# One sequence for the first layer: three groups of row-tiled products in place of four, and an earlier transfer of the second half's remainder

## Chip, cores and metric

The kernel runs on one core of one Trainium2 chip; the other cores are idle. The metric is the device time of one execution, in microseconds (us), as the median of several runs. "The span" is the time from the first to the last instruction of one execution taken with the hardware profiler.

## What is computed

Six cross layers over a batch of 4096 rows of 416 features, all in bf16:

```python
def reference(x0, ws, bs):          # x0 4096 x 416, ws 6 x 416 x 416, bs 6 x 416
    x = x0
    for l in range(ws.shape[0]):
        x = x0 * (x @ ws[l] + bs[l]) + x
    return x
```

## The kernel before

**Layout.** For layers 0 to 4 the features lie on the partitions. 416 is three blocks of 128 (`XM`, index `k` as input and `m` as output) and a remainder of 32 (`XR`). The batch is cut into two halves `s` of 2048 rows, each half into four groups `g` of 512. Since 32 features fill a quarter of the partitions only, `XR` keeps the four groups of a half on top of each other: group `g` sits on partitions `32g` to `32g+31`. A second copy, `XRd`, holds the same with its lower and upper 64 partitions exchanged. `XM[0]` and `XR[0]` hold x0; layer 0 writes `XM[1]` and `XR[1]`.

**Products on PE.** An output of 128 features x 1024 rows (a half-block: half `s`, block `m`, `h` = which two of the four groups) is one PSUM tile of two banks, called `ph` in layer 0 and `pt` in layers 1 to 4. It needs three *full* products for each of its two groups (128 x 128 weights, `k` = 0, 1, 2; L233), and one *row-tiled* product for each group, whose 32 input features take one quarter of the rows of the array (L240). Four row-tiled products in the four different quarters run side by side; this is one round. Output block `m = 1` reads `XRd` instead of `XR[0]`, so that its two products fall into the two quarters which the others leave free. In layers 1 to 4 the main products are *column-tiled* (L200): four products of 32 output features each run side by side and make one round. The remainder's own 32 outputs are column-tiled as well (`mm_rem`, L212 and L217, tile `pr`).

**After PE.** ACT reads a finished PSUM tile, adds the bias and writes `t` in bf16 (L173). DVE multiplies `t` by x0 (L180) and adds x (L183); for the remainder L189 and L192. There are four PSUM tiles of two banks and six `t` buffers, each given out again when its last reader is done.

**The first layer before the change.** `first_layer(s)` runs once for each half. The half begins with the three half-blocks of `h = 0` (`pa`), then comes a group of eight row-tiled products (two rounds), then the three half-blocks of `h = 1` (`pb`), then a group of four (one round). After the second half, `mm_rem` makes the remainder's outputs for both halves in one tile `pr`, and layer 1 starts with the tile pair of `s = 0, m = 0`: `mm_full` for groups 0 and 1 into the first tile of the pair, groups 2 and 3 into the second, then `mm_row`.

**Where the remainder of x0 comes from.** For the first half, four transfers bring it to `xrig` (L83); PE turns it into the tile `tpr` (L159), and DVE copies that to `XR[0]` and twice, by halves, to `XRd` (L162). For the second half, one transfer brings it to `xrem` (`load_xrem1`, L88, on ACT's queue); DVE transposes it to `XR[0]` in blocks of 32 x 32 (L167) and makes two copies to `XRd` (L169). The transfer is kept back by a tiny DVE write to `xrem` (L86), which stands behind the copies of L162 and which the transfer must wait for. The remainder rows of the first layer's weights come by one transfer to 32 partitions of `WR`, and are copied to the other three quarters by ACT (twice, L115) and POOL (L117). Eight transposing transfers on SP's queue (L75) bring x0 to `XM[0]`, one for each group of 512 rows.

`pin` keeps an instruction in the order in which it is written, on its engine. ACT, DVE and PE each take their instructions in one order.

Of the kernel before, what the change touches and what calls it, by code (L numbers as in the profile page):

```python
# [9 lines left out]
ACT = mybir.ActivationFunctionType  # L10
ALU = mybir.AluOpType
BF16 = mybir.dt.bfloat16
# [4 lines left out]
def kernel(  # L17
# [7 lines left out]
    nc = tc.nc  # L25
    B, D = x0.shape
    L = ws.shape[0]
    P = 128
    NK = 3
    R = D - NK * P  # L30
    assert R == 32 and B == 4096 and D == 416 and L >= 2
    NS = 2
    NG = 4
    CW = 512
# [6 lines left out]
    tpool = ctx.enter_context(tc.tile_pool(name="tpool", bufs=6))  # L41
    opool = ctx.enter_context(tc.tile_pool(name="opool", bufs=10))
    psum = ctx.enter_context(tc.tile_pool(name="psum", bufs=4, space=bass.MemoryType.PSUM))
# [7 lines left out]
    WM = const.tile([P, L, NK, D], BF16)  # L51
    WR = const.tile([P, L, D], BF16)
# [3 lines left out]
    bM = const.tile([P, NK, L], FP32)  # L56
    bR = const.tile([P, L], FP32)
# [3 lines left out]
    xrem = big.tile([P, 16, R], BF16)  # L61
    xrig = big.tile([P, 4, P], BF16)
    XRd = big.tile([P, NS * CW], BF16)
    XM = [big.tile([P, NK, B], BF16, name=f"XM{i}") for i in range(3)]
    XR = [big.tile([P, NS * CW], BF16, name=f"XR{i}") for i in range(3)]

    def col0(s, g):
        return SW * s + CW * g
# [8 lines left out]
    def pin(ins):  # L77
        tc.keep_in_program_order(ins)
# [3 lines left out]
            for i in range(4):  # L82
                nc.scalar.dma_start(xrig[:, i, :].rearrange("p (g r) -> p g r", g=NG), x0_v[:, i:16:4, NK * P:D])  # L83

    def load_xrem1():
        pin(nc.vector.memset(xrem[:, 0, 0:1], 0.0))  # L86
        with nc.allow_non_contiguous_dma(reason="64B row segments"):
            pin(nc.scalar.dma_start(xrem[:], x0[SW:2 * SW, NK * P:D].rearrange("(p t) r -> p t r", p=P)))  # L88

# [19 lines left out]
    load_xrem0()  # L109
    load_wr0()  # L110
    nc.scalar.activation(dz[:, 1:2], dz[:, 0:1], ACT.Identity, bias=dz[:, 0:1], scale=1.0)  # L111
    for g in range(1, NG):
        dst, src = WR[32 * g:32 * g + 32, 0, :], WR[0:R, 0, :]
        if g < NG - 1:
            nc.scalar.copy(dst, src)  # L115
        else:
            nc.gpsimd.tensor_copy(dst, src)  # L117
    for g in range(2, NG):
        load_x0t(0, g)
    load_x0t(1, 0)  # L120
# [13 lines left out]
    def fill_wd(l0, l1):  # L134
        for g in range(NG):
            nc.gpsimd.tensor_copy(WD[32 * g:32 * g + 32, l0:l1, g, :], WR[32 * g:32 * g + 32, l0:l1, NK * P:D])

    fill_wd(0, 1)
    fill_wd(1, L)

    wps = psum.tile([P, CW], FP32, tag="ps", name="wps")

# [13 lines left out]
    def x0_rem0(tpr):  # L156
        nc.tensor.transpose(tpr[:, CW:CW + L], bsb[0:L, NK * P:4 * P], ident[0:L, 0:L])
        for i in range(4):
            nc.tensor.transpose(tpr[:, 128 * i:128 * i + 128], xrig[:, i, :], ident[:])  # L159
        for dst, src in ((slice(0, P), slice(0, P)), (slice(64, P), slice(0, 64)), (slice(0, 64), slice(64, P))):  # L160
            to = XR[0] if dst == src else XRd
            pin(nc.vector.tensor_copy(to[dst, 0:CW], tpr[src, 0:CW]))  # L162
        nc.vector.tensor_copy(bR[:], tpr[:, CW:CW + L])
        load_xrem1()

    def x0_rem1():
        pin(nc.vector.transpose(XR[0][:, CW:2 * CW].rearrange("p (j t) -> p t j", t=16), xrem[:]))  # L167
        for dst, src in ((slice(64, P), slice(0, 64)), (slice(0, 64), slice(64, P))):
            pin(nc.vector.tensor_copy(XRd[dst, CW:2 * CW], XR[0][src, CW:2 * CW]))  # L169

    def ew_act(n, pt, bias):
        t = tpool.tile([P, 2 * CW], BF16, name="t")
        nc.scalar.activation(t[:, 0:n], pt, ACT.Identity, bias=bias, scale=1.0)  # L173
        return t

    def ew_main(l, s, m, h, pt, cur, nxt, pin_all=False, t=None):
        c0 = col0(s, 2 * h)
        if t is None:
            t = ew_act(2 * CW, pt[:].rearrange("p a b -> p (a b)"), bM[:, m, l:l + 1])
        prod = nc.vector.tensor_tensor(out=t[:], in0=t[:], in1=XM[0][:, m, c0:c0 + 2 * CW], op=ALU.mult)  # L180
        if pin_all:
            pin(prod)
        total = nc.vector.tensor_tensor(out=nxt[:, m, c0:c0 + 2 * CW], in0=t[:], in1=cur[:, m, c0:c0 + 2 * CW], op=ALU.add)  # L183
        if pin_all and s:
            pin(total)

    def ew_rem(l, s, pr, curR, nxtR, pin_all=False, t=None):
        tr = ew_act(CW, pr, bR[:, l:l + 1]) if t is None else t
        prod = nc.vector.tensor_tensor(out=tr[:, 0:CW], in0=tr[:, 0:CW], in1=XR[0][:, CW * s:CW * s + CW], op=ALU.mult)  # L189
        if pin_all:  # L190
            pin(prod)
        total = nc.vector.tensor_tensor(out=nxtR[:, CW * s:CW * s + CW], in0=tr[:, 0:CW], in1=curR[:, CW * s:CW * s + CW], op=ALU.add)  # L192
        if pin_all:
            pin(total)

    def mm_full(l, s, m, g, pts, cur, first, last):
        c0 = col0(s, g)
        for k in range(NK):
            for q in range(4):
                nc.tensor.matmul(pts[g // 2][32 * q:32 * q + 32, g % 2, :], lhsT=WM[:, l, k, 128 * m + 32 * q:128 * m + 32 * q + 32],  # L200
                                 rhs=cur[:, k, c0:c0 + CW], start=(first and k == 0), stop=(last and k == NK - 1),
                                 tile_position=(0, 32 * q))

    def mm_row(l, s, m, pts, curR, first, last):
        for g in range(NG):
            nc.tensor.matmul(pts[g // 2][:, g % 2, :], lhsT=WR[32 * g:32 * g + 32, l, 128 * m:128 * m + 128],  # L206
                             rhs=curR[32 * g:32 * g + 32, CW * s:CW * s + CW],
                             start=first, stop=last, tile_position=(32 * g, 0))

    def mm_rem(l, s, pr, cur, curR):  # L210
        for g in range(NG):
# [12 lines left out]
        nc.sync.dma_start_transpose(out=XLrows[:, 16 * s:16 * s + 16, 128 * k:128 * k + 128],  # L224
                                    in_=nxt[:, k, SW * s:SW * s + SW])

    def first_layer(s):
        cur, curR, nxt, nxtR = XM[0], XR[0], XM[1], XR[1]

        def full(pt, m, h, gl, after_row):  # L230
            c0 = col0(s, 2 * h + gl)
            for k in range(NK):
                nc.tensor.matmul(pt[:, gl, :], lhsT=WM[:, 0, k, 128 * m:128 * m + 128], rhs=cur[:, k, c0:c0 + CW],  # L233
                                 start=(k == 0 and not after_row), stop=(k == NK - 1 and after_row))

        def row(pt, m, h, opens):
            for gl in range(2):
                rg = 32 * ((2 * h + gl) ^ (2 if m == 1 else 0))
                src = XRd if m == 1 else curR
                nc.tensor.matmul(pt[:, gl, :], lhsT=WR[rg:rg + 32, 0, 128 * m:128 * m + 128],  # L240
                                 rhs=src[rg:rg + 32, CW * s:CW * s + CW],
                                 start=opens, stop=not opens, tile_position=(rg, 0))

        def ph(m):
            return psum.tile([P, 2, CW], FP32, tag="ps", name=f"ph{m}")

        pa = [ph(m) for m in range(NK)]
        if s == 0:
            for m in range(NK):
                full(pa[m], m, 0, 0, False)  # L250
            tp0 = psum.tile([P, CW + 8], BF16, tag="ps", name="tpr")
            x0_rem0(tp0[:])
            for m in range(NK):
                full(pa[m], m, 0, 1, False)
        else:
            for gl in range(2):
                for m in range(NK):
                    full(pa[m], m, 0, gl, False)
        pb = [ph(0)]
        row(pa[0], 0, 0, False)  # L260
        row(pb[0], 0, 1, True)
        row(pa[2], 2, 0, False)
        row(pa[1], 1, 0, False)
        for m in range(NK):
            ew_main(0, s, m, 0, pa[m], cur, nxt, pin_all=(s == 1))
        for m in range(NK):
            if m:
                pb.append(ph(m))
            for gl in range(2):
                full(pb[m], m, 1, gl, m == 0)  # L270
        row(pb[1], 1, 1, False)
        row(pb[2], 2, 1, False)
        if s == 0:
            x0_rem1()
            for m in range(NK):
                ew_main(0, s, m, 1, pb[m], cur, nxt, pin_all=True)
            return
        pr = psum.tile([P, 2, CW], FP32, tag="ps", name="pr")
        for r in range(NS):
            mm_rem(0, r, pr[:, r, :], cur, curR)  # L280

        def act_main(m):
            return ew_act(2 * CW, pb[m][:].rearrange("p a b -> p (a b)"), bM[:, m, 0:1])

        tb, tr = [act_main(0), act_main(1)], [ew_act(CW, pr[:, 0, :], bR[:, 0:1])]
        tb.append(act_main(2))
        tr.append(ew_act(CW, pr[:, 1, :], bR[:, 0:1]))
        ew_rem(0, 0, None, curR, nxtR, True, tr[0])
        for m in range(NK):
            ew_main(0, s, m, 1, None, cur, nxt, True, tb[m])  # L290
        ew_rem(0, 1, None, curR, nxtR, True, tr[1])

    bias_setup()
    pe_filler(1, CW)
    for s in range(NS):
        first_layer(s)

    def rem_pair(l, cur, curR, nxtR, feeds_last):
        pr2 = psum.tile([P, 2, CW], FP32, tag="ps", name="pr2")
# [13 lines left out]
    for l in range(1, LL):  # L313
# [3 lines left out]
        pts = {}  # L317
# [136 lines left out]
```

## Time and profile before

| | |
|---|---|
| Runs | 130.12, 130.23, 130.55 us; median 130.23 |
| The profiled execution | 130.03 us, of which the span is 128.2 us |
| Granted TensorE clock, mean | 0.995 |
| PE busy | 122.7 us (96%), 1698 products |
| DVE busy | 108.1 us (84%), 196 instructions |
| ACT busy | 86.8 us (68%), 99 instructions |
| DMA | 16.38 MB in 42230 packets, 31034 of them under 512 B |

The share of busy time of PE says only that its products follow each other; the chain of waits says whether another engine holds it up. The profile page gives for each line of the kernel (L233 and so on) the number of instructions, the busy time, the mean duration, and the idle time before them with what ended it.

### The profile page before, as it was taken

Reading aid. Unit: us, or ns where it says so; the run is one execution under the profiler, and the core shown is the slowest. Engines: PE = TensorE matmul, PEld = TensorE weight load, DVE = VectorE, ACT = ScalarE, POOL = GpSimd, SP = SyncE. Lnnn points to the kernel's source line nnn. Section 1 sums busy time; section 2 is a strip of 40 time slices with the busy share of each in tenths; the row PEclk is TensorE's granted clock in tenths of the full one; section 3 lists DMA queues with packets and bytes.
Section 4 is the critical chain, followed back from the end, with each engine's and each line's share of the span. In section 5 each row is a group of like instructions: output and inputs, shape, how many; then the busy total and the mean of one; then the engine's idle time right before and its main releaser. Section 6 shows DMA issues by size and latency. Waiting matters only on the chain.

```text
span 128.2 us, 3995 instructions
## 1 busy us (share of the span) xinstructions
PE 122.7 (96%) x1698; PEld 55.1 (43%) x1698; DVE 108.1 (84%) x196; ACT 86.8 (68%) x99; POOL 5.5 (4%) x18
## 2 busy tenths in 40 slices
PE   7999999999999999999999999999999999999960
PEld 3344343444344444434444434444434445445420
DVE  0033999999999999999999989898989899898991
ACT  0138857878496658857658857658857897569670
POOL 4004000700000000000000000000000000000000
PEclk9999999999999999999999999999999999999997
DMA  3999999999960000000000000000297899987754
GB/s 93 248 233 196 193 222 251 279 332 332 337 202 0 5 0 8 0 0 5 0 5 0 5 0 5 0 0 5 48 160 165 161 134 240 182 269 248 224 183 136
DMA packets 42230, 16.38 MB, mean 128 GB/s; under 512 B 31034, under 2 KB 42212, under 8 KB 42212
## 3 DMA queue, kind: packets, MB, share of 16 engines
q1 hardware_dynamic: 37432, 15.40, 52.8%
q10 hardware_dynamic: 4780, 0.72, 3.7%
q8 instruction: 13, 0.21, 0.7%
q14 instruction: 5, 0.04, 0.1%
HBM read 6.15 MB, written 3.41 MB: 75 GB/s over the span
## 4 chain that ended last, share of the span: by engine, by line
PE 81%; DVE 6%; DMA 6%; ACTq 2%; issue 1%; SPq 1%; ACT 1%; DVEq 0%
PE pt L200 50%; PE ph L233 11%; PE pt L206 5%; PE pr L217 5%; PE py L365 4%; DMA xrig<-in_x_dram 4%; DVE t L393 4%; DVE o L382 2%; DMA out_dram<-o 2%; PE pr L212 2%; PE ph L240 1%; PE py L360 1%; ACTq L83 1%; SPq L383 1%; PE py L371 1%
## 5 line engine op out<-in xcount | busy, mean ns | idle before, releaser
L200 PE MATMUL pt<-XM,WM 128*32 128x512 bf16 x1152 | 65.2, 379 | 0.0
L173 ACT ACTIVATE t<-pt,bM 128x1024 bf16<-128x1024 f32 x48 | 49.6, 1115 | 17.7 <-PE pt L206 17.7
L183 DVE TENSOR_TENSOR XM<-t,XM 128x1024 bf16<-128x1024 bf16 x60 | 41.5, 692 | 3.6
L180 DVE TENSOR_TENSOR t<-t,XM 128x1024 bf16<-128x1024 bf16 x60 | 41.4, 689 | 3.5 <-ACT t L173 3.4
L200 PEld LDWEIGHTS <-WM 128*32 128x32 bf16 x1152 | 29.7, 97 | 33.8 <-issue 5.1
L392 ACT CAST t<-py 128x416 bf16<-128x416 f32 (+1 forms) x23 | 14.8, 643 | 4.7 <-PE py L365 2.5
L233 PE MATMUL ph<-XM,WM 128*128 128x512 bf16 x72 | 16.4, 379 | 0.3 <-DMA XM<-in_x_dram 0.3
L365 PE MATMUL py<-WM,XM 128*128 128x416 bf16 x90 | 16.5, 339 | 0.0
L173 ACT ACTIVATE t<-ph,bM 128x1024 bf16<-128x1024 f32 x12 | 12.6, 1113 | 3.5 <-PE ph L240 3.5
L365 PEld LDWEIGHTS <-XM 128*128 128x128 bf16 x90 | 8.5, 98 | 7.8 <-issue 1.4
L393 DVE TENSOR_TENSOR t<-t,X0rows 128x416 bf16<-128x416 bf16 (+1 forms) x23 | 10.4, 456 | 1.1 <-ACT t L392 1.1
L233 PEld LDWEIGHTS <-WM 128*128 128x128 bf16 x72 | 6.8, 98 | 8.8 <-issue 1.3
L382 DVE TENSOR_TENSOR o<-t,XLrows 128x416 bf16<-128x416 bf16 (+1 forms) x23 | 10.4, 455 | 0.0
L173 ACT ACTIVATE t<-pr,bR 128x512 bf16<-128x512 f32 x10 | 6.4, 685 | 2.9 <-PE pr L217 2.9
L217 PE MATMUL pr<-XM,WM 128*32 128x512 bf16 x120 | 8.2, 379 | 0.0
L206 PE MATMUL pt<-XR,WR 32*128 32x512 bf16 x96 | 7.3, 379 | 0.0
L111 ACT ACT_TABLE_LOAD x1 | 1.3, 1283 | 6.0 <-DMA XM<-in_x_dram 6.0
L192 DVE TENSOR_TENSOR XR<-t,XR 128x512 bf16<-128x512 bf16 x10 | 4.2, 424 | 0.7
L217 PEld LDWEIGHTS <-WM 128*32 128x32 bf16 x120 | 3.2, 97 | 3.2
L145 PE MATMUL wps<-const-float32-1.0 128*128 128x512 f32 x4 | 3.6, 1044 | 0.8 <-PEq L438 0.8
L189 DVE TENSOR_TENSOR t<-t,XR 128x512 bf16<-128x512 bf16 x10 | 4.2, 419 | 0.0
L154 DVE CAST bM<-pb 128x18 f32<-128x18 bf16 x1 | 0.2, 177 | 4.5 <-PE pb L153 4.5
(42 smaller groups left out, 36.7 us busy)
## 6 DMA issues: line engine op xcount, KB each, us to landing
X0rows<-in_x_dram SPq DMA_DIRECT2D x8, 312.0 KB, 7.1
out_dram<-o SPq DMA_DIRECT2D x9, 208.0 KB, 4.2
WM<-in_ws_dram SPq DMA_DIRECT2D x5, 312.0 KB
out_dram<-o SPq DMA_DIRECT2D x13, 104.0 KB, 1.7
X0rows<-in_x_dram SPq DMA_DIRECT2D x4, 208.0 KB, 6.1
WR<-in_ws_dram SPq DMA_DIRECT2D x4, 130.0 KB, 5.2
WM<-in_ws_dram ACTq DMA_DIRECT2D x1, 312.0 KB
XM<-in_x_dram SPq DMA_TRANSPOSE x8, 5.6
```

Source lines behind the costliest of these rows:

```text
L173: nc.scalar.activation(t[:, 0:n], pt, ACT.Identity, bias=bias, scale=1.0)
L180: prod = nc.vector.tensor_tensor(out=t[:], in0=t[:], in1=XM[0][:, m, c0:c0 + 2 * CW], op=ALU.mult)
L183: total = nc.vector.tensor_tensor(out=nxt[:, m, c0:c0 + 2 * CW], in0=t[:], in1=cur[:, m, c0:c0 + 2 * CW], op=ALU.add)
L189: prod = nc.vector.tensor_tensor(out=tr[:, 0:CW], in0=tr[:, 0:CW], in1=XR[0][:, CW * s:CW * s + CW], op=ALU.mult)
L200: nc.tensor.matmul(pts[g // 2][32 * q:32 * q + 32, g % 2, :], lhsT=WM[:, l, k, 128 * m + 32 * q:128 * m + 32 * q + 32], rhs=cur[:, k, c0:c ...
L206: nc.tensor.matmul(pts[g // 2][:, g % 2, :], lhsT=WR[32 * g:32 * g + 32, l, 128 * m:128 * m + 128], rhs=curR[32 * g:32 * g + 32, CW * s:CW ...
L217: nc.tensor.matmul(pr[32 * g:32 * g + 32, :], lhsT=WM[:, l, k, NK * P:D], rhs=cur[:, k, c0:c0 + CW], start=False, stop=(k == NK - 1), tile ...
L233: nc.tensor.matmul(pt[:, gl, :], lhsT=WM[:, 0, k, 128 * m:128 * m + 128], rhs=cur[:, k, c0:c0 + CW], start=(k == 0 and not after_row), sto ...
L365: nc.tensor.matmul(py[:, 0:D], lhsT=cur[:, k, q_cols(q, g)], rhs=WM[:, l, k, :], start=((not closes) and k == 0), stop=(closes and k == NK ...
L382: tc.keep_in_program_order(nc.vector.tensor_tensor(out=o, in0=t, in1=xl, op=ALU.add))
L392: nc.scalar.copy(tv, src)
L393: tc.keep_in_program_order(nc.vector.tensor_tensor(out=tv, in0=tv, in1=X0rows[:, b, :], op=ALU.mult))
```

## The change

The two calls of `first_layer(s)` become one call that issues all twelve half-blocks of layer 0 in one sequence. Its row-tiled products stand in three groups of eight (two rounds each). The second group, issued after 24 full products, holds the last ones of the first half (`pb[1]`, `pb[2]`) and the first ones of the second half (`qa[0]`, `qa[1]`). The third holds the rest. The last half-block (`qb[2]`: s = 1, m = 2, h = 1) is issued after the third group with column-tiled products (`cols`), and `mm_rem` follows it. Most instructions of the first layer, and the products of layer 1's first pair, are pinned.

The tiny DVE write that releases the transfer of `xrem` becomes a copy of one column out of `tpr`, and it moves ahead of the three copies to `XR[0]` and `XRd`. The transfer moves ahead of the two copies of `WR` on ACT's queue. DVE's transpose of `xrem` moves from behind the sixth elementwise instruction of layer 0 to behind the second. One of the two copies to `XRd` that follow it goes to ACT (`x0_rem1_low`). ACT's order at the end of the layer is: tile `qa[2]`, `qb[0]`, first remainder, `qb[1]`, `qb[2]`, second remainder. On DVE the first remainder moves ahead of the half-block `qa[2]`.

```diff
-    def load_xrem1():
-        pin(nc.vector.memset(xrem[:, 0, 0:1], 0.0))
+    def load_xrem1(tpr):
+        pin(nc.vector.tensor_copy(xrem[:, 0, 0:1], tpr[:, 3 * P:3 * P + 1]))
         with nc.allow_non_contiguous_dma(reason="64B row segments"):
             pin(nc.scalar.dma_start(xrem[:], x0[SW:2 * SW, NK * P:D].rearrange("(p t) r -> p t r", p=P)))
...
             nc.tensor.transpose(tpr[:, 128 * i:128 * i + 128], xrig[:, i, :], ident[:])
+        load_xrem1(tpr)
+        copy_wr0()
         for dst, src in ((slice(0, P), slice(0, P)), (slice(64, P), slice(0, 64)), (slice(0, 64), slice(64, P))):
             to = XR[0] if dst == src else XRd
             pin(nc.vector.tensor_copy(to[dst, 0:CW], tpr[src, 0:CW]))
         nc.vector.tensor_copy(bR[:], tpr[:, CW:CW + L])
-        load_xrem1()
 
     def x0_rem1():
         pin(nc.vector.transpose(XR[0][:, CW:2 * CW].rearrange("p (j t) -> p t j", t=16), xrem[:]))
-        for dst, src in ((slice(64, P), slice(0, 64)), (slice(0, 64), slice(64, P))):
-            pin(nc.vector.tensor_copy(XRd[dst, CW:2 * CW], XR[0][src, CW:2 * CW]))
+        pin(nc.vector.tensor_copy(XRd[64:P, CW:2 * CW], XR[0][0:64, CW:2 * CW]))
+
+    def x0_rem1_low():
+        pin(nc.scalar.copy(XRd[0:64, CW:2 * CW], XR[0][64:P, CW:2 * CW]))
...
+        def cols(pt, s, m, h, gl):
+            c0 = col0(s, 2 * h + gl)
+            for k in range(NK):
+                for q in range(4):
+                    pin(nc.tensor.matmul(pt[32 * q:32 * q + 32, gl, :], lhsT=WM[:, 0, k, 128 * m + 32 * q:128 * m + 32 * q + 32],
+                                         rhs=cur[:, k, c0:c0 + CW], start=False, stop=(k == NK - 1), tile_position=(0, 32 * q)))
...
+        dve_main(0, 0, 0, act_main(pa[0], 0))
+        x0_rem1()
+        for m in range(1, NK):
+            dve_main(0, m, 0, act_main(pa[m], m))
...
+        qa = [ph(m) for m in range(2)]
+        for m in range(2):
+            full(qa[m], 1, m, 0, 0, True)
+        row(pb[1], 0, 1, 1, ())
+        row(pb[2], 0, 2, 1, ())
+        row(qa[0], 1, 0, 0, (1,))
+        row(qa[1], 1, 1, 0, (1,))
+        for m in range(1, NK):
+            dve_main(0, m, 1, act_main(pb[m], m))
+        for m in range(2):
+            full(qa[m], 1, m, 0, 1, False)
+            dve_main(1, m, 0, act_main(qa[m], m))
+        x0_rem1_low()
+        qa.append(ph(2))
+        qb = []
+        for gl in range(2):
+            full(qa[2], 1, 2, 0, gl, True)
+        for m in range(2):
+            qb.append(ph(m))
+            for gl in range(2):
+                full(qb[m], 1, m, 1, gl, True)
+        qb.append(ph(2))
+        row(qa[2], 1, 2, 0, ())
+        row(qb[0], 1, 0, 1, ())
+        row(qb[1], 1, 1, 1, ())
+        row(qb[2], 1, 2, 1, (0, 1))
+        ta, tb = act_main(qa[2], 2), [act_main(qb[0], 0)]
+        for gl in range(2):
+            cols(qb[2], 1, 2, 1, gl)
         pr = psum.tile([P, 2, CW], FP32, tag="ps", name="pr")
         for r in range(NS):
             mm_rem(0, r, pr[:, r, :], cur, curR)
+        tr = [act_rem(0)]
+        tb += [act_main(qb[1], 1), act_main(qb[2], 2)]
+        tr.append(act_rem(1))
         ew_rem(0, 0, None, curR, nxtR, True, tr[0])
+        dve_main(1, 2, 0, ta)
         for m in range(NK):
-            ew_main(0, s, m, 1, None, cur, nxt, True, tb[m])
+            dve_main(1, m, 1, tb[m])
         ew_rem(0, 1, None, curR, nxtR, True, tr[1])
```

More of the change, by code (lines that the diff above doesn't have):

```diff
@@ L111 @@
     nc.scalar.activation(dz[:, 1:2], dz[:, 0:1], ACT.Identity, bias=dz[:, 0:1], scale=1.0)
[L112 to L117, printed above, removed]
     for g in range(2, NG):
@@ L136, in fill_wd, with copy_wr0 @@
             nc.gpsimd.tensor_copy(WD[32 * g:32 * g + 32, l0:l1, g, :], WR[32 * g:32 * g + 32, l0:l1, NK * P:D])
-    fill_wd(0, 1)
-    fill_wd(1, L)
+    def copy_wr0():
+        for g in range(1, NG):
+            dst, src = WR[32 * g:32 * g + 32, 0, :], WR[0:R, 0, :]
+            if g < NG - 1:
+                pin(nc.scalar.copy(dst, src))
+            else:
+                nc.gpsimd.tensor_copy(dst, src)
+        fill_wd(0, 1)
+        fill_wd(1, L)
     wps = psum.tile([P, CW], FP32, tag="ps", name="wps")
@@ L199, in mm_full @@
             for q in range(4):
-                nc.tensor.matmul(pts[g // 2][32 * q:32 * q + 32, g % 2, :], lhsT=WM[:, l, k, 128 * m + 32 * q:128 * m + 32 * q + 32],
-                                 rhs=cur[:, k, c0:c0 + CW], start=(first and k == 0), stop=(last and k == NK - 1),
-                                 tile_position=(0, 32 * q))
+                mm = nc.tensor.matmul(pts[g // 2][32 * q:32 * q + 32, g % 2, :], lhsT=WM[:, l, k, 128 * m + 32 * q:128 * m + 32 * q + 32],
+                                      rhs=cur[:, k, c0:c0 + CW], start=(first and k == 0), stop=(last and k == NK - 1),
+                                      tile_position=(0, 32 * q))
+                if (l, s, m) == (1, 0, 0):
+                    pin(mm)
     def mm_row(l, s, m, pts, curR, first, last):
         for g in range(NG):
-            nc.tensor.matmul(pts[g // 2][:, g % 2, :], lhsT=WR[32 * g:32 * g + 32, l, 128 * m:128 * m + 128],
-                             rhs=curR[32 * g:32 * g + 32, CW * s:CW * s + CW],
-                             start=first, stop=last, tile_position=(32 * g, 0))
+            mm = nc.tensor.matmul(pts[g // 2][:, g % 2, :], lhsT=WR[32 * g:32 * g + 32, l, 128 * m:128 * m + 128],
+                                  rhs=curR[32 * g:32 * g + 32, CW * s:CW * s + CW],
+                                  start=first, stop=last, tile_position=(32 * g, 0))
+            if (l, s, m) == (1, 0, 0):
+                pin(mm)
     def mm_rem(l, s, pr, cur, curR):
@@ L225, in xl_dmat, with first_layer, ph, full @@
                                     in_=nxt[:, k, SW * s:SW * s + SW])
-    def first_layer(s):
+    def first_layer():
         cur, curR, nxt, nxtR = XM[0], XR[0], XM[1], XR[1]
-        def full(pt, m, h, gl, after_row):
+        def ph(m):
+            return psum.tile([P, 2, CW], FP32, tag="ps", name=f"ph{m}")
+        def full(pt, s, m, h, gl, opens, held=True):
             c0 = col0(s, 2 * h + gl)
             for k in range(NK):
-                nc.tensor.matmul(pt[:, gl, :], lhsT=WM[:, 0, k, 128 * m:128 * m + 128], rhs=cur[:, k, c0:c0 + CW],
-                                 start=(k == 0 and not after_row), stop=(k == NK - 1 and after_row))
-        def row(pt, m, h, opens):
+                mm = nc.tensor.matmul(pt[:, gl, :], lhsT=WM[:, 0, k, 128 * m:128 * m + 128], rhs=cur[:, k, c0:c0 + CW],
+                                      start=(opens and k == 0), stop=(not opens and k == NK - 1))
+                if held:
+                    pin(mm)
+        def cols(pt, s, m, h, gl):
[4 more added lines that the diff above has]
+                                         rhs=cur[:, k, c0:c0 + CW], start=False, stop=(k == NK - 1), tile_position=(0, 32 * q)))
+        def row(pt, s, m, h, opens):
             for gl in range(2):
@@ L239, in row @@
                 src = XRd if m == 1 else curR
[L240 to L245, printed above, removed]
-        pa = [ph(m) for m in range(NK)]
[L248 to L255, printed above, removed]
-            for gl in range(2):
-                for m in range(NK):
-                    full(pa[m], m, 0, gl, False)
@@ L259, in first_layer @@
[L259 to L268, printed above, removed]
-            for gl in range(2):
[L270 to L277, printed above, removed]
+                pin(nc.tensor.matmul(pt[:, gl, :], lhsT=WR[rg:rg + 32, 0, 128 * m:128 * m + 128],
+                                     rhs=src[rg:rg + 32, CW * s:CW * s + CW],
+                                     start=gl in opens, stop=gl not in opens, tile_position=(rg, 0)))
@@ new lines, in act_main, with act_rem, dve_main @@
+        def act_main(pt, m):
+            t = tpool.tile([P, 2 * CW], BF16, name="t")
+            pin(nc.scalar.activation(t[:], pt[:].rearrange("p a b -> p (a b)"), ACT.Identity, bias=bM[:, m, 0:1], scale=1.0))
+            return t
+        def act_rem(r):
+            t = tpool.tile([P, 2 * CW], BF16, name="t")
+            pin(nc.scalar.activation(t[:, 0:CW], pr[:, r, :], ACT.Identity, bias=bR[:, 0:1], scale=1.0))
+            return t
+        def dve_main(s, m, h, t):
+            ew_main(0, s, m, h, None, cur, nxt, True, t)
@@ new lines, in first_layer @@
+        pa = [ph(m) for m in range(NK)]
+        for m in range(NK):
+            full(pa[m], 0, m, 0, 0, True, held=False)
+        tp0 = psum.tile([P, CW + 8], BF16, tag="ps", name="tpr")
+        x0_rem0(tp0[:])
+        for m in range(NK):
+            full(pa[m], 0, m, 0, 1, True, held=False)
+        pb = [ph(0)]
+        row(pa[0], 0, 0, 0, ())
+        row(pb[0], 0, 0, 1, (0, 1))
+        row(pa[2], 0, 2, 0, ())
+        row(pa[1], 0, 1, 0, ())
+        dve_main(0, 0, 0, act_main(pa[0], 0))
@@ new lines, in first_layer @@
+        x0_rem1()
+        for m in range(1, NK):
+            dve_main(0, m, 0, act_main(pa[m], m))
+        for gl in range(2):
+            full(pb[0], 0, 0, 1, gl, False)
+        dve_main(0, 0, 1, act_main(pb[0], 0))
+        for m in range(1, NK):
+            pb.append(ph(m))
+            for gl in range(2):
+                full(pb[m], 0, m, 1, gl, True)
+        qa = [ph(m) for m in range(2)]
+        for m in range(2):
+            full(qa[m], 1, m, 0, 0, True)
+        row(pb[1], 0, 1, 1, ())
@@ new lines, in first_layer @@
+        row(pb[2], 0, 2, 1, ())
+        row(qa[0], 1, 0, 0, (1,))
+        row(qa[1], 1, 1, 0, (1,))
+        for m in range(1, NK):
+            dve_main(0, m, 1, act_main(pb[m], m))
[9 more added lines that the diff above has]
+            qb.append(ph(m))
+            for gl in range(2):
+                full(qb[m], 1, m, 1, gl, True)
@@ L280, in first_layer @@
             mm_rem(0, r, pr[:, r, :], cur, curR)
[L282 to L287, printed above, removed]
+        tr = [act_rem(0)]
+        tb += [act_main(qb[1], 1), act_main(qb[2], 2)]
+        tr.append(act_rem(1))
         ew_rem(0, 0, None, curR, nxtR, True, tr[0])
+        dve_main(1, 2, 0, ta)
         for m in range(NK):
-            ew_main(0, s, m, 1, None, cur, nxt, True, tb[m])
+            dve_main(1, m, 1, tb[m])
         ew_rem(0, 1, None, curR, nxtR, True, tr[1])
@@ L294 @@
     pe_filler(1, CW)
-    for s in range(NS):
-        first_layer(s)
+    first_layer()
     def rem_pair(l, cur, curR, nxtR, feeds_last):
```

## The prediction

> **What bounds the kernel now.** I read the chain of waits first, since PE is busy 96% of the span and the question is whether anything else paces it. In the first layer the chain lies on PE from 8.55 us on, without a gap:
>
> ```profile
> 8.55 2.09 PE ph L233 x9
> 10.64 0.62 PE ph L240 x8
> 11.27 3.99 PE ph L233 x18
> 15.26 0.33 PE ph L240 x4
> 15.58 3.99 PE ph L233 x18
> 19.57 0.54 PE ph L240 x8
> 20.12 3.99 PE ph L233 x18
> 24.11 0.33 PE ph L240 x4
> 24.44 0.33 PE pr L212 x4
> 24.77 0.65 PE pr L217 x12
> 25.41 0.22 PE pr L212 x4
> 25.63 0.65 PE pr L217 x12
> 26.28 2.59 PE pt L200 x48
> ...
> 29.41 5.29 PE pt L200 x96
> ```
>
> The columns are start, duration, engine, tile, line, count. It stays on PE until 111 us, and the tail of DVE work and output transfers behind that hangs on PE's last tiles. So a us that PE loses or saves in the first layer moves the end by a us. The list of PE's own waits shows only 0.3 us for data (the first block of x0); there is nothing else to save on PE but the products and what lies between them.
>
> Second, DVE in order of time, around the remainder of the second half:
>
> ```profile
> 9.92 0.17 DVE L163 CAST bR<-tpr 128x6 f32<-128x6 bf16 x1
> 10.03 0.06 DVE L86 MEMSET xrem<- 128x1 bf16 x1
> ...
> 16.42 2.36 DVE L167 STREAM_TRANSPOSE XR<-xrem 128x512 bf16<-128x512 bf16 x1 [0.19 <-DMA xrem<-in_x_dram]
> 18.81 0.61 DVE L169 COPY XRd<-XR 64x512 bf16<-64x512 bf16 x2
> ```
>
> The transfer is issued at 10.14 and has landed by 16.4 (6.3 us by the list of transfers). DVE starts on it at once. The result is complete at 19.4, just ahead of its first use on PE at 19.57.
>
> Third, ACT at the change to layer 1:
>
> ```profile
> 24.47 1.11 ACT L173 ACTIVATE t<-ph,bM 128x1024 bf16<-128x1024 f32 x1 [0.41 <-PE ph L240]
> 26.33 0.69 ACT L173 ACTIVATE t<-pr,bR 128x512 bf16<-128x512 f32 x1 [0.74 <-PE pr L217]
> 26.92 1.11 ACT L173 ACTIVATE t<-ph,bM 128x1024 bf16<-128x1024 f32 x1
> 27.91 0.69 ACT L173 ACTIVATE t<-pr,bR 128x512 bf16<-128x512 f32 x1
> ```
>
> The first remainder (26.33) starts only when PE is through with *both* halves of `pr` (26.28), although its own half was ready at 25.41; ACT stood idle for 0.74 us.
>
> **What the change saves.** A round takes 0.216 us, full or column-tiled (2.59 / 12 for L200). A change of tiling costs 0.11: two rounds of row-tiled products take 0.54 = 2 x 0.216 + 0.11, one takes 0.33, 18 full ones behind them 3.99 = 18 x 0.216 + 0.10, and the first L212 behind rows takes 0.33 against 0.22. From 11.27 to 26.28 PE now needs 15.01. After: 24 full (5.29, as the 24 rounds of L200 x96), rows 0.54, 24 full 5.29, rows 0.54, the last half-block column-tiled 6 x 0.216 + 0.11 = 1.41, remainder 0.22 + 0.65 + 0.22 + 0.65 = 1.74; sum 14.81. Two changes of tiling fewer: **-0.20 us**. The rounds stay the same number, so the column-tiled half-block itself costs nothing.
>
> **First new wait: the remainder of the second half.** Rows of the second half now stand in the second group. Without waits it starts at 11.27 + 5.29 = 16.56, its second round (`qa[0]`, `qa[1]`) at 16.56 + 0.33 = 16.89, and it ends at 17.10. Before, these rows came at 19.57, so the need is 2.7 us earlier. The transfer moves less. DVE has `tpr` at 8.59. The one-column copy lies between the memset's 0.06 and the 0.17 of the 128x6 cast out of the same tile; I take 0.17, the row that reads PSUM too. It ends at 8.76 and the issue follows 0.05 later, as now (10.09 to 10.14): 8.81, which is 1.33 earlier.
>
> How long the transfer then takes, I bound by 4.1 us (each of the four `xrig` transfers, a quarter of its size, 64 B pieces too) and by 6.8 (its own 6.3 and a margin of half a us, if it gets no breathing space between two transposing transfers of SP). Its own row is nearest: then as now it is issued beside a transposing transfer, with the DMA engines' share around or above 1 in nearly every us (1.28, 0.80, 1.17, 0.78, 1.23, 1.33 from 9 to 15 us). I take 6.1: landed at 14.9.
>
> The Trainium skill ("DMA: Bandwidth & Descriptors", Anatomy of one DMA) fits a transfer issued by GpSimd with 2.0 us and its bytes at 436 GB/s; for these 128 KB that is an estimate of 2.3 us, by which the wait would be gone and the sum +0.30. The row of this very transfer, 6.3, disagrees and decides.
>
> DVE is free by then (idle from 13.6, after the first half-block), and the transpose cannot start before the landing: 14.93 + 2.36, copy 0.03 behind it and 0.29 long, complete at 17.61. PE's last row pair then starts at 17.65 and ends at 17.87 instead of 17.10: **+0.77 us**. In general the wait is landing - 14.13, and nothing for a landing before that; from 0 (4.1 us) to 1.5 (6.8 us).
>
> Queued behind the waiting row pair are the six full products of `qa`'s second group (1.29 us), which need no remainder. The Trainium skill ("TensorE: Matmul & The Clock Gate", Step-by-step: what each phase is for) says that PE pulls weight loads ahead but keeps products in order; no row here shows it. By the opposite these six would fill the wait and it would cost nothing.
>
> **Second new wait: a PSUM tile for layer 1.** When `mm_rem` runs, `qa[2]`, `qb[0]`, `qb[1]`, `qb[2]` have held all four tiles. `pr` gets that of `qa[2]`, layer 1's first pair those of `qb[0]` and `qb[1]`. ACT's order is `qa[2]`, `qb[0]`, first remainder, `qb[1]`, ..., and the first remainder waits for all of `pr`. So ACT is through with `qb[0]` some 2 us after the third group, idles until `pr` ends, takes the remainder (next start 0.59 later, as 26.33 to 26.92) and then 1.11 for `qb[1]`: done 0.05 + 0.59 + 1.11 = 1.75 after the end of `pr`. PE comes to the pair's second tile 6 x 0.216 = 1.30 after it. Wait **+0.50 us** with 0.05 for the signal. Before, the tile in that place was read by 25.58 and PE came at 27.6. The only escape is a first remainder that starts on its own half, 0.87 earlier; the 0.74 us of idle ACT above speak against it. The next pair needs the tiles of `qb[2]` and `pr`: ACT ends those 2.74 and 3.31 after `pr`; PE, by its wait, comes at 0.50 + 2.59 + 0.33 = 3.42. Just covered.
>
> **Edits that I cost at nothing.** The `WR` copies stand behind the transfer's issue (0.64 long, 8.81 to 9.45); they wait for their own data until 9.51 anyway (cover 0.06; if gone, the first rows, which already took 0.62 instead of 0.54, slip by as much). POOL's copy waits for the same data. DVE's copies to `XR[0]` and `XRd` slip by 0.17 and end at 10.07; rows start at 10.64. On SP's queue the fifth transposing transfer (landed at 12.93, needed at 15.27) now runs beside `xrem`, the sixth (16.6, needed behind the wait, after 17.1) less so. ACT's copy to `XRd` must be done for the third group, over 5 us later. DVE idles 1.3 us ahead of the transpose, and 0.4 for the first remainder; it must have `XR[1]` of the second half for layer 1's second row group. From the end of the copy it needs 11 pairs of 1.33, two remainder pairs of 0.8, one pair of layer 1, 1.33, and the idle 0.4: 17.61 + 18.0 = 35.6. PE needs it at 28.8 - 0.2 + 0.77 + 0.50 + 5.9 + 0.33 = 36.1. Cover 0.5.
>
> **Sum.** -0.20 + 0.77 + 0.50 = +1.07 on the profiled execution's 130.03 (span 128.2 and 1.83 around it). It lies 0.20 under the median of 130.23; I forecast medians: 130.23 + 1.07 = **131.3 us**. A measurement of this kernel can tell some 0.3% (0.39 us) from no change.
>
> **Rivals.**
> *The transfer lands by 14.13*, in 5.3 us or less, which lies between the rows of 4.1 and 6.3. For it: the last of four `xrig` transfers, together of its size, landed 4.1 us after its own issue, among the same neighbours. Against it: its own row. Then only the PSUM wait is left: +0.30, 130.5, no measurable change. Chance 0.11.
> *Not slower: ACT takes the first remainder as soon as its half is ready* and the transfer lands by 14.13. `qb[1]` is then read 0.87 earlier and the PSUM wait (0.50) is gone; the saving stands alone: 130.0. It decides only if both hold; the early start is contradicted by the trace, and the landing needs over 1 us less than the same transfer took. Should the saved changes of tiling count double, it would reach 129.8. Chance 0.06, of it 0.03 for faster than 0.39.
> *PE passes the waiting rows*: +0.30, 130.5. Chance 0.03.
> *The transposing transfers suffer*: `xrem` pushes the sixth past its need, over 1 us later than now. Each us beyond is one more on PE: up to 132.3. Against it: the same packets are moved in the same time by then. Chance 0.06.
> *The forecast*: both waits, landing between 14.25 and 15.6, +0.4 to +1.8. Chance 0.74.
>
> So slower 0.80, same 0.17, faster 0.03. The range runs from just under the first rival, 130.4, to a landing at 15.6, 131.9.
>
> **What would show it.** In the changed profile: three groups of L260 with 0.54 each and the two saved changes of tiling; PE waiting at about 17 us for DVE's transpose and copy, with the length landing - 14.13; a wait of 0.5 us at the second tile of layer 1's first pair, ended by ACT; the chain on PE elsewhere. It is wrong if `xrem` lands before 14.1 or PE runs through the change to layer 1.

## The result

The changed kernel takes 130.95 us (median of six runs, 130.86 to 131.34) where the kernel before takes 130.23: 1.006 times as long, with a 95% interval of 1.0046 to 1.0074, which is 0.6 to 1.0 us more. The profiled execution is the slowest of the six, 131.34 us with a span of 129.5 us. Its granted clock is 0.996 (0.995 before), DVE's and ACT's busy times are the same within half a us, and the same 16.38 MB are moved in as many packets.

The chain of waits of the changed kernel, from the first row group to layer 1 (start, duration, engine, tile, line, count; L244 full, L260 row-tiled, L253 column-tiled, L220 and L225 the remainder, L204 and L212 layer 1; on ACT L271 is a remainder and L266 a half-block; "issue" is time in which the engine waited for nothing that the profile shows):

```profile
10.97 0.69 PE ph L260 x8
11.66 5.29 PE ph L244 x24
16.95 0.99 PE ph L260 x8
17.94 5.29 PE ph L244 x24
23.22 0.54 PE ph L260 x8
23.77 1.41 PE ph L253 x24
25.18 0.22 PE pr L220 x4
25.39 0.65 PE pr L225 x12
26.04 0.22 PE pr L220 x4
26.25 0.68 PE pr L225 x12
26.93 0.02 issue
26.96 0.69 ACT t L271
27.64 1.01 ACT t L266
28.66 0.04 issue
28.70 1.48 PE pt L204 x24
30.18 0.54 PE pt L212 x8
```

Three things are new. The first row group ends at 11.66, 0.39 later than before (11.27). The second takes 0.99 us where the third takes 0.54: 0.45 us of waiting. And the chain leaves PE between 26.93 and 28.70, for two activations of ACT, in the midst of layer 1's first pair; from the end of `pr` to layer 1's row group it is 30.18 - 26.93 = 3.25 us, and 28.87 - 26.28 = 2.59 before.

DVE in order of time shows whom the second row group waits for (start, duration, engine, line, operation, tiles, count; in brackets the idle time before and what ended it):

```profile
14.83 2.34 DVE L169 STREAM_TRANSPOSE XR<-xrem 128x512 bf16<-128x512 bf16 x1 [0.93 <-DMA xrem<-in_x_dram]
17.21 0.29 DVE L170 COPY XRd<-XR 64x512 bf16<-64x512 bf16 x1
```

DVE stood idle for 0.93 us until the transfer had landed at 14.8; its copy is complete at 17.50, and PE's last row pair starts at 17.55. ACT in order of time shows the other wait:

```profile
9.12 0.62 ACTq L88 DMA_DIRECT2D xrem<-in_x_dram  x1
...
26.96 0.69 ACT L271 ACTIVATE t<-pr,bR 128x512 bf16<-128x512 f32 x1 [1.25 <-PE pr L225]
27.54 2.11 ACT L266 ACTIVATE t<-ph,bM 128x1024 bf16<-128x1024 f32 x2
```

ACT idles for 1.25 us until both halves of `pr` are done, takes the first remainder, and only then reads `qb[1]`, whose tile PE needs. PE in order of time names it:

```profile
28.70 1.48 PE L204 MATMUL pt<-XM,WM 128*32 128x512 bf16 x24 [0.50 <-ACT t L266]
```

### The profile page after: what moved, and what is told of

Same layout as the page of the kernel before. It is cut to its first block, busy times and chain, and to the rows that moved or that the text cites. A ratio compares the mean times of both kernels' runs of the same rounds, so it can differ in the third digit from the quotient of the medians.

```text
span 129.5 us, 4032 instructions
## 1 busy us (share of the span) xinstructions
PE 123.8 (96%) x1716; PEld 55.6 (43%) x1716; DVE 107.7 (83%) x195; ACT 87.3 (67%) x100; POOL 4.6 (4%) x18
## 2 busy tenths in 40 slices
DMA packets 42230, 16.38 MB, mean 126 GB/s; under 512 B 31034, under 2 KB 42212, under 8 KB 42212
## 4 chain that ended last, share of the span: by engine, by line
PE 85%; DVE 7%; ACT 2%; DMA 2%; issue 1%; DVEq 0%
PE pt L204 48%; PE ph L244 11%; PE pt L212 5%; PE pr L225 5%; DVE t L440 4%; PE py L412 4%; PE wps L146 4%; DVE o L429 3%; DMA out_dram<-o 2%; PE ph L260 2%; PE pr L220 2%; PE ph L253 1%; PE py L407 1%; ACT t L266 1%; PE py L418 1%
## 5 line engine op out<-in xcount | busy, mean ns | idle before, releaser
L204 PE MATMUL pt<-XM,WM 128*32 128x512 bf16 x1152 | 65.4, 379 | 0.5 <-ACT t L266 0.5
L177 ACT ACTIVATE t<-pt,bM 128x1024 bf16<-128x1024 f32 x48 | 49.6, 1115 | 17.4 <-PE pt L212 17.4
L204 PEld LDWEIGHTS <-WM 128*32 128x32 bf16 x1152 | 29.7, 97 | 34.3 <-issue 5.7
L439 ACT CAST t<-py 128x416 bf16<-128x416 f32 (+1 forms) x23 | 14.8, 643 | 4.7 <-PE py L412 2.5
L266 ACT ACTIVATE t<-ph,bM 128x1024 bf16<-128x1024 f32 x12 | 12.5, 1114 | 3.7 <-PE ph L260 3.7
L244 PE MATMUL ph<-XM,WM 128*128 128x512 bf16 x66 | 14.9, 379 | 0.0
L244 PEld LDWEIGHTS <-WM 128*128 128x128 bf16 x66 | 6.2, 98 | 7.6 <-issue 0.7
L225 PE MATMUL pr<-XM,WM 128*32 128x512 bf16 x120 | 8.2, 379 | 0.0
L212 PE MATMUL pt<-XR,WR 32*128 32x512 bf16 x96 | 7.3, 379 | 0.0
L177 ACT ACTIVATE t<-pr,bR 128x512 bf16<-128x512 f32 x8 | 5.1, 684 | 2.1 <-PE pr L225 2.1
L225 PEld LDWEIGHTS <-WM 128*32 128x32 bf16 x120 | 3.2, 97 | 3.3
```

The lines of the kernel that those rows point to most:

```text
L204: mm = nc.tensor.matmul(pts[g // 2][32 * q:32 * q + 32, g % 2, :], lhsT=WM[:, l, k, 128 * m + 32 * q:128 * m + 32 * q + 32], rhs=cur[:, k, ...
L212: mm = nc.tensor.matmul(pts[g // 2][:, g % 2, :], lhsT=WR[32 * g:32 * g + 32, l, 128 * m:128 * m + 128], rhs=curR[32 * g:32 * g + 32, CW * ...
L225: nc.tensor.matmul(pr[32 * g:32 * g + 32, :], lhsT=WM[:, l, k, NK * P:D], rhs=cur[:, k, c0:c0 + CW], start=False, stop=(k == NK - 1), tile ...
L244: mm = nc.tensor.matmul(pt[:, gl, :], lhsT=WM[:, 0, k, 128 * m:128 * m + 128], rhs=cur[:, k, c0:c0 + CW], start=(opens and k == 0), stop=( ...
L266: pin(nc.scalar.activation(t[:], pt[:].rearrange("p a b -> p (a b)"), ACT.Identity, bias=bM[:, m, 0:1], scale=1.0))
L439: nc.scalar.copy(tv, src)
```

## The experiments

Theory A is that of the prediction: two changes of tiling saved, and two new waits on PE, each of which counts in full. The rivals are named with each run. Seven kernels and the changed one again ran beside the kernel before (130.21 and 130.25 us in the two sets).

**ACT reads `qb[1]` first (e1_act_order).**

```diff
+        tb.append(act_main(qb[1], 1))
         tr = [act_rem(0)]
-        tb += [act_main(qb[1], 1), act_main(qb[2], 2)]
+        tb.append(act_main(qb[2], 2))
```

> The changed kernel, with ACT reading qb[1] ahead of the first remainder. Theory A (each of the two new waits holds up PE, and they add): the wait of 0.50 us at the second tile of layer 1's first pair is gone, the wait at the second row group stays; 0.5 us under the changed kernel, some 130.45 us. Rival B (the PSUM wait only hides the next late one: DVE's first remainder, or the tiles of the second pair, are late by as much): PE waits somewhere behind it, and the time stays near 130.95.

Measured: 130.62 us, 1.0032 times the kernel before (1.0017 to 1.0047), 0.33 under the changed kernel. The profiled execution is the slowest of the twelve, 131.33 us; its transfer of `xrem` took longer, which is taken up further down. The wait of 0.50 is gone from the list of PE's waits, but 0.2 us come back 8 us later, as rival B said in part. PE and its weight loads in order of time, at layer 1's second row group:

```profile
35.61 0.82 PE L212 MATMUL pt<-XR,WR 32*128 32x512 bf16 x8
...
36.03 0.10 PEld L212 LDWEIGHTS <-WR 32*128 32x128 bf16 x4 [0.33 <-DVE XR L196]
```

The group takes 0.82 instead of 0.61 (both with the overlap of the last products): its second half waits for DVE's last write to `XR[1]`. With PE sooner there, the cover of 0.5 us that the prediction gave to DVE is used up.

**DVE makes the second remainder sooner (e5_rem_sooner, on top of e1).**

```diff
-        for m in range(NK):
+        for m in range(2):
             dve_main(1, m, 1, tb[m])
         ew_rem(0, 1, None, curR, nxtR, True, tr[1])
+        dve_main(1, 2, 1, tb[2])
```

> The kernel of e1_act_order, with DVE making the second remainder ahead of the last half-block qb[2] instead of behind it. In e1 the eight row-tiled products of layer 1's second group took 0.82 us instead of 0.61, with the weight load waiting for DVE's last write of XR[1]. Theory A (that is where 0.2 of e1's 0.5 us went): 0.61 us again and some 0.2 us under e1, 130.4 us. Rival B (something else is late there too): stays at 130.6.

Measured: 130.51 us, ratio 1.0011 (0.9992 to 1.0031). The row group is back at 0.61:

```profile
35.10 0.61 PE L212 MATMUL pt<-XR,WR 32*128 32x512 bf16 x8
```

The medians of e1 and e5 differ by 0.11 us only, and their intervals overlap; the row settles it, not the times. Taken together, the two edits give back 0.44 to 0.58 us of the changed kernel's time (130.95 and 131.09 in its two sets).

**The transfer of `xrem` released by a plain memset (e2_release_memset).**

```diff
-        pin(nc.vector.tensor_copy(xrem[:, 0, 0:1], tpr[:, 3 * P:3 * P + 1]))
+        pin(nc.vector.memset(xrem[:, 0, 0:1], 0.0))
```

> The changed kernel, with the transfer of xrem released by a memset that waits for nothing of PE, so that ACT issues it right behind its first activation, some 1.2 us sooner than in the changed kernel. Theory A: it lands before 14.1 us on the clock of the prediction, the second row group takes 0.54 us instead of 0.99, and the time is 0.45 us under the changed kernel, some 130.5 us; the PSUM wait of 0.50 stays. Rival C (all transfers share the DMA engines, so the transposing transfers of x0 pay): PE waits for x0 blocks ahead of the second row group and the gain is lost, 130.95 or more.

Measured: 131.46 us, ratio 1.0094 (1.0081 to 1.0107), 0.4 to 0.5 us slower than the changed kernel in its two sets. The issue came at 7.29 us, the transfer was there when DVE wanted it, and the second row group took 0.54. But PE in order of time:

```profile
12.96 4.69 PE L244 MATMUL ph<-XM,WM 128*128 128x512 bf16 x20 [0.72 <-DMA XM<-in_x_dram]
```

PE waits 0.72 us for the fourth block of x0, for which it did not wait in the kernel before. That block landed 5.9 us after its issue (6.97 to 12.9); in the changed kernel it took 4.1 us (7.05 to 11.13 by the records of the trace). The wait for `xrem` is gone and a longer one for its neighbour has come: rival C.

**The transfer put back to its old place (e3_release_late).**

```diff
-        load_xrem1(tpr)
         copy_wr0()
...
         nc.vector.tensor_copy(bR[:], tpr[:, CW:CW + L])
+        load_xrem1(tpr)
```

> The changed kernel, with the issue of xrem's transfer put back behind the copies to XR[0] and XRd, and behind the WR copies, as before. Theory A (the wait at the second row group is landing plus 2.7 us, one for one): issue 1.2 to 1.3 us later, as much more waiting, 132.1 to 132.3 us. Rival D (the DMA engines set the landing, not the issue): landing and time move by less than half a us.

Measured: 134.14 us (133.36 to 135.14), ratio 1.0305 (1.0261 to 1.0348); neither theory gave so much. The chain of waits:

```profile
10.50 6.30 DMA xrem<-in_x_dram
...
16.82 2.33 DVE XR L169
...
19.20 0.76 PE ph L260 x4
19.95 6.88 PE ph L244 x24
```

The issue is 1.4 us later than in the changed kernel and the landing 2.0, since the transfer now takes 6.3 us and not 5.7; the second row group ends 2.0 us later (19.95 for 17.94). The row group ends 3.1 us after the landing, as in the changed kernel (14.81 and 17.94; the prediction had 2.9); so far theory A holds. The rest is in the last line: the 24 full products take 6.88 us, 1.6 more than the 5.29 in the other profiles that have them in one row. The table by stretches (length, then busy time and count of PE, PEld, DVE, ACT and POOL, granted clock, DMA share, GB/s) shows why:

```profile
18.00:19.00 1.00, 0.00 (x0) 0.00 (x0) 1.00 (x1) 1.00 (x2) 0.00 (x0) 1.00 1.19 256
...
20.00:21.00 1.00, 1.00 (x3) 0.31 (x3) 0.97 (x3) 0.00 (x0) 0.00 (x0) 0.50 1.13 277
21.00:22.00 1.00, 1.00 (x4) 0.31 (x3) 0.96 (x2) 0.62 (x1) 0.40 (x1) 0.50 1.20 240
22.00:23.00 1.00, 1.00 (x4) 0.44 (x3) 0.96 (x3) 0.83 (x2) 0.94 (x2) 0.50 1.01 228
23.00:24.00 1.00, 1.00 (x6) 0.39 (x4) 1.00 (x2) 0.97 (x2) 0.14 (x1) 0.92 1.06 313
```

After 2.23 us without a product (16.97 to 19.20) the granted clock fell to 0.50 for some 3.4 us. It did not in every run: the mean granted clock is 0.984 to 0.987 in the three runs of 134.71 to 135.14 us, the profiled one among them, and 0.996 to 0.999 in the three of 133.36 to 133.56. The prediction had no such term; its own waits are shorter.

**The last half-block with full products (e4_last_full).**

```diff
-            cols(qb[2], 1, 2, 1, gl)
+            full(qb[2], 1, 2, 1, gl, False)
```

> The changed kernel, with the last half-block of layer 0 made of full products in place of column-tiled ones: one more change of tiling on PE. By the price read from the chain, 0.11 us more, 131.05 us; by the rival that a change between full and column-tiled costs nothing, 130.95.

Measured: 131.16 us, ratio 1.0062 (1.0043 to 1.0081); the changed kernel had 1.0060 and 1.0065, so the times cannot tell 0.1 us. The chain of waits can:

```profile
23.24 0.54 PE ph L260 x8
23.79 0.16 issue
23.95 1.24 PE ph L244 x5
25.19 0.33 PE pr L220 x4
25.52 0.65 PE pr L225 x12
```

From the end of the rows to L225 it is 25.52 - 23.79 = 1.73 us, against 25.39 - 23.77 = 1.62 with column-tiled products: 0.11 more. The six full products with the change ahead of them take 25.19 - 23.79 = 1.40 us, as long as the column-tiled ones; the chain has five of them and 0.16 of "issue", since the record of one is missing (their six weight loads are there). The 0.11 sits in L220 (0.33 for 0.22), the first column-tiled products behind full ones. So a change between full and column-tiled costs as much as the others, in this one profile.

**The release between the two (e6_gate_xrig, on top of e5).**

```diff
-        pin(nc.vector.tensor_copy(xrem[:, 0, 0:1], tpr[:, 3 * P:3 * P + 1]))
+        pin(nc.vector.tensor_copy(xrem[:, 0, 0:1], xrig[:, 2, 0:1]))
```

> The kernel of e5_rem_sooner, with the one-column copy that releases the transfer of xrem taken from xrig's third part instead of from tpr, so that it waits for a landing and not for PE: issue some 0.4 to 0.6 us sooner, between the changed kernel's and that of e2_release_memset. Theory A: the second row group's wait shrinks by as much and is gone, the two saved changes of tiling are left, 130.0 us, 0.2 under the kernel before. Rival C (the transposing transfers pay, as the fourth one did in e2 by 0.72 us): PE waits for x0 at the start of qb's or pb's products instead, 130.4 or more.

Measured: 130.00 us, ratio 0.9985 (0.9974 to 0.9996): the only version whose interval lies below the kernel before. The issue came at 8.42 us; DVE went from its first half-block straight to the transpose:

```profile
13.63 2.35 DVE L169 STREAM_TRANSPOSE XR<-xrem 128x512 bf16<-128x512 bf16 x1
```

and the chain of waits has no wait from the first row group to layer 1:

```profile
11.46 1.62 PE ph L244 x7
...
16.74 0.54 PE ph L260 x8
17.28 5.29 PE ph L244 x24
22.57 0.54 PE ph L260 x8
...
26.25 2.59 PE pt L204 x48
```

From 11.46 to 26.25 PE needs 14.79 us, against 15.01 before: the two saved changes of tiling, alone at last. In this profile the transfer took 5.1 us (8.42 to 13.51 by the records of the trace), so it was quick as well as early. With the 5.9 us of e1 and e4 it would have landed at 14.3, and the row group would have ended at 17.4 instead of 17.28; this is an estimate from the 3.1 us between landing and end in the other profiles.

**Three full products ahead of the rows (e7_three_ahead, on top of e5).**

```diff
             full(qa[m], 1, m, 0, 0, True)
+        full(qa[0], 1, 0, 0, 1, True)
         row(pb[1], 0, 1, 1, ())
...
-        row(qa[0], 1, 0, 0, (1,))
+        row(qa[0], 1, 0, 0, ())
...
+        full(qa[1], 1, 1, 0, 1, False)
         for m in range(2):
-            full(qa[m], 1, m, 0, 1, False)
             dve_main(1, m, 0, act_main(qa[m], m))
```

> The kernel of e5_rem_sooner, with three of the six full products behind the second row group (qa[0], second group of rows of x0) moved ahead of it. Theory A: the rows come 0.65 us later and the wait of 0.45 for xrem is gone; but qa[2] then waits for ACT to read pb[1], which starts only with the rows: 0.2 us; together 0.2 to 0.25 under e5, 130.2 us. Rival (the six products behind the rows are no cover, PE just idles there): same as e5.

Measured: 130.25 us, ratio 1.0007 (0.9994 to 1.0020), a median 0.26 under e5, as theory A has it; but the ratios of the two differ by 0.0004 only, so the times do not show it. The chain of waits shows what is left of both waits:

```profile
17.27 0.74 PE ph L260 x8
18.00 0.75 PE ph L244 x3
18.76 0.04 issue
18.80 4.05 PE ph L244 x18
```

The row group still takes 0.20 too long; in this profile the transfer took 6.0 us (issue at 8.84). The three products behind it hold the usual change of tiling (0.75 for 3 x 0.216 = 0.65). Then PE pauses for 0.04, and the next 18 take 4.05 for 18 x 0.216 = 3.89: the new wait costs 0.20, as expected.

**The changed kernel again (a1_after_again).**

> The changed kernel again, on the chip and in the rounds of the three others: 130.95 us, 0.7 over the kernel before.

Measured: 131.09 us, ratio 1.0065 (1.0048 to 1.0081). Its profiled execution, 131.12 us, differs from the first one in a way that matters below. The chain on PE, then DVE:

```profile
11.27 0.66 PE ph L260 x8
11.92 1.62 PE ph L244 x7
...
17.21 0.54 PE ph L260 x8
```

```profile
14.61 2.35 DVE L169 STREAM_TRANSPOSE XR<-xrem 128x512 bf16<-128x512 bf16 x1 [0.42 <-DMA xrem<-in_x_dram]
```

Here PE came to the end of the first row group only at 11.92. The transfer took 5.2 us (issue at 9.37, landing at 14.59) where it took 5.7 in the first profile, and the second row group did not wait at all; it ended at 17.75, where the first profile had 17.94.

## Why the prediction was right, and where it was off

The sign and the range held: 130.95 and 131.09 lie between 130.4 and 131.9. (A landing at 15.6 gives 130.23 + 0.30 + 1.47 = 132.0; the range's upper end is 0.1 short of its own condition.) The wait for a PSUM tile is in both profiles of the changed kernel, the wait for `xrem` in one of the two. The centre, 131.3, was 0.2 to 0.35 too high. The sum was made for one profiled execution, so it is compared first with the two that were taken of the changed kernel. Their terms are differences of times on the chain:

| term | predicted | first profile | second profile |
|---|---|---|---|
| end of the first row group, less 11.27 | 0 | +0.39 | +0.65 |
| two changes of tiling | -0.20 | -0.19 | -0.18 |
| wait for `xrem` | +0.77 | +0.45 | 0 |
| wait for the PSUM tile, L204's first pair less 2.59 | +0.50 | +0.66 | +0.65 |
| sum | +1.07 | +1.31 | +1.12 |
| profiled time less 130.03 | | +1.31 | +1.09 |

That the second profile's sum is so near +1.07 is luck: a late first row group, which the prediction did not have, stands in place of a wait that did not come.

*The saving* was right: 14.79 us in e6 for 14.81 predicted. The price of 0.11 for a change of tiling also holds between full and column-tiled products (e4), which the kernel before did not show.

*The wait for a PSUM tile* was right in its cause and in the length of the gap, 0.50, but it costs 0.66: the 24 products behind the gap take 1.48 us instead of 6 x 0.216 = 1.30. A single product lasts 0.379 us by the profile's means, and the next one ends 0.216 later, since they overlap; the first one behind a gap has nothing to overlap with, and 0.379 - 0.216 = 0.16. The same 0.16 stands behind other gaps: in e2 the four products behind the wait for x0 take 1.02 us instead of 0.86, in e7 18 take 4.05 instead of 3.89. The prediction left this out, in the other wait too: it gave the waiting row pair 0.22 us (17.65 to 17.87), and the pair took 0.39 (17.55 to 17.94). The wait is gone when ACT's order is changed (e1), and its cause is confirmed by that; the time that e1 and e5 gave back, 0.44 to 0.58, is somewhat under 0.66, with e5's runs scattered from 129.72 to 130.84. The first remainder did wait for all of `pr` (ACT idle for 1.25 us), so the rival on the other side stayed shut.

*The wait for `xrem`* is the term that was mis-sized: 0.45 and nothing. What failed in it is the time of the transfer: 6.1 us were taken, from the 6.3 of the kernel before, and 5.7 and 5.2 came. The versions that keep this part of the order show the same law (the wait is the time from the end of the first row group to the end of the second, less 5.29 + 0.54):

| profile | end of the first row group | transfer, issue to landing | wait |
|---|---|---|---|
| changed kernel, first | 11.66 | 5.69 | 0.45 |
| changed kernel, second | 11.92 | 5.21 | 0 |
| e1 | 11.75 | 5.93 | 0.71 |
| e4 | 11.37 | 5.94 | 0.76 |
| e5 | 11.42 | 5.77 | 0.53 |

The wait is the transfer's time less 5.2 us; the prediction's own numbers make it 6.1 - 0.77 = 5.3. It does not become shorter when PE is late at its start, because the release hangs on PE too: the one-column copy reads `tpr`, so the issue is late by as much. The chain in e1 has the hand-over:

```profile
8.76 0.24 PE tpr L160
...
9.03 0.07 DVE xrem L86
...
9.23 5.93 DMA xrem<-in_x_dram
```

The prediction's rule, landing - 14.13, is bound to PE's times in the kernel before: the landings at 14.81 and 14.59 would make it 0.68 and 0.46. That the end of the row group came out so well (17.87, measured 17.94 and 17.75) is luck in part: in the first profile an issue 0.31 later (9.12) and the missing 0.16 make up for a transfer that was 0.4 shorter. The first rival, a transfer of 5.3 us or less, has its condition on the transfer fulfilled in one of the two profiles, with a landing at 14.59 and not by 14.13; it had been given 0.11.

From this follows where the centre went wrong. The wait for `xrem` was forecast 0.32 to 0.77 too long, the wait for the PSUM tile 0.16 too short: by the two profiles the sum is 0.16 to 0.61 too high, and by the medians 0.2 to 0.35. The late first row group adds in full. Most of it arises ahead of the rows: the nine full products before them start at 8.89 and 9.16 instead of 8.55, in the second profile behind a wait of 0.50 us for a transfer to `xrig`. How much of such lateness the median of the kernel before holds is not known, since it has one profile; so the 0.20 added for the median stays argued, not shown.

*The edits at nothing* held, with little to spare: DVE's cover of 0.5 us for `XR[1]` was real, as e1 showed by using it up. The `WR` copies, for which the prediction allowed a cover of 0.06, cost 0.07 more than before at the most: the first rows behind them take 0.64 to 0.69 us in the two profiles and those of e5, e6 and e7, against 0.62 before.

*The other rivals.* That PE passes waiting rows is refuted: in e3 six full products stood for 2.2 us behind the waiting pair, and the block of x0 that they read had landed at 16.83 (by the records of the trace), before the pause. The Trainium skill ("TensorE: Matmul & The Clock Gate", Step-by-step: what each phase is for) says that products stay in program order, and here the trace agrees. That the transposing transfers suffer did not happen with the issue at 9.1 us, and did at 7.3 (0.72 us, e2). Between them, at 8.4, PE waits for neither (e6).

## What to carry to other kernels

When work is moved up on the engine that sets the time, look up the producer of every operand and ask whether it moves by as much; here the rows came 2.7 us sooner and their transfer's issue only 0.8 to 1.0 in the two profiles. An order written out for one engine (ACT's) is also the order in which buffers come free for another (PE's): list who holds each buffer when the next one is asked for. And when the engine that waits for a transfer also releases it, the wait hangs on the transfer's own time: the profile of the kernel before gave 6.3 us, and the others 5.1 to 6.3, so it has to be forecast as a range.

## What was not expected of the hardware

A pause of 2.23 us in TensorE's products was followed by about 3.4 us at a granted clock of 0.50 (e3), which cost 1.6 us on top of the pause; by the mean clocks this came in three of six runs of the same kernel. Pauses of up to 0.72 us (e2) had no such effect in the profiles. The Trainium skill ("TensorE: Matmul & The Clock Gate", What's actually happening) names an idle window of about 3.4 us for such a fall; here 2.2 us were enough, and the measurement decides for this case. Second, a transfer in pieces of 64 B that is issued at 7.29 us (e2) made PE wait 0.72 us for a transposing transfer whose issue had begun before it, at 6.97. Third, one and the same transfer of 128 KB took between 5.1 and 6.3 us from profile to profile (6.3 in the kernel before and e3, 5.1 in e6); what sets it was not found.
